# Low parts of the experts' weights by accumulating DMAs instead of subtractions in a Fourier filter with a mixture of experts

## The chip, the cores and the metric

The kernel runs on one core of a Trainium2 chip. The metric is the time of one execution on the device in microseconds (us). The names of the engines are those of the profile: PE is TensorE (PEld its weight loads), DVE is VectorE, ACT is ScalarE, POOL is GpSimd, SP is SyncE, which here only issues DMAs. ACT and POOL issue DMAs as well.

## What is computed

Eight sequences of 3072 tokens with 256 channels are filtered by a circular convolution (a real Fourier transform, a product with a filter, the transform back). The result, 24576 tokens, goes through a mixture of 8 experts: each token goes to the expert with the largest logit, an expert takes its first 768 tokens, and each token that was kept leaves as its gate weight times the expert's two-layer network. All other rows of the output are zero.

```python
X = np.fft.rfft(x, axis=1)
y = np.fft.irfft(X * (filt_r + 1j * filt_i)[None], n=x.shape[1], axis=1)
x = y.reshape(B * S, D)
logits = x @ w_gate                      # 8 experts
expert_idx = np.argmax(logits, axis=1)   # disp[e]: the first 768 rows of expert e
h = np.maximum(np.einsum('ecd,edf->ecf', disp, w1), 0.0)   # 256 -> 1024
y = np.einsum('ecf,efd->ecd', h, w2)                       # 1024 -> 256
out[i] = gate_w[i] * y[expert_idx[i], pos[i]]              # rows that were kept
```

## The kernel before

The convolution is worked out for three of the eight batches only, since the experts are full by then (a guarded second path does the rest if they are not). A batch goes through `Conv.a` and `t` (the forward transform), then `middle`, which works through six groups `g` of frequencies: `b` multiplies by the filter (DVE L267, POOL L271 and L272), `g` and `bi` transform back. `ti` and `ai` finish the transform; `ai` copies its banks to tiles `rt` (five buffers, ACT L355) and writes them to DRAM (`ybuf`, SP L359). `route` works out on DVE which token stands in which slot of which expert. In the third batch `middle` also takes pieces of other work from the list `fill`.

The experts follow. An expert has 768 slots, worked on as two chunks of 384. `prep` turns a chunk's rows, which indirect DMAs on POOL have gathered (L485), and splits them into a high part rounded to fp32r (`xh`) and a low part, the remainder (`xl`). `up` makes the hidden layer: eight steps of six matmuls of 384 columns, for the three products high by high, high by low and low by high over two halves of the 256 channels (L532, operands `wah`, `wal`, `xh`, `xl`). After each step ACT rounds the bank to the high part of `h` (L507) and DVE makes its low part (L515). `down` has three steps of 24 matmuls of 256 columns (L584, with `wbh` and `wbl`), after which ACT scales the bank into a tile `ob` (L587, four buffers) and POOL scatters its rows by an indirect DMA (L588). Matmul results go through seven PSUM banks.

The weights are split the same way, and this is what the change touches. `load_part` (L606) loads one matrix of one expert, 1 MB, as tile `raw` (part "a" is w1 with two rows of 1024 values on a partition, part "b" is w2 with eight rows of 256). It gives back the load and a list of cuts. A cut rounds its share of the columns to the high part on ACT (L621) and subtracts the high part from `raw` on POOL (L622), in one case on DVE. Experts 0 and 1a are cut into four pieces a matrix (512 columns), the later ones into two (1024 columns). There is one `raw` buffer at first (`raw0`), two later. Where the cuts stand:

- expert 0, part a: in `fill` of the third batch's `middle` (L786 to L788), one piece each in four places; the gathers of the first rows (`early_rows`) stand between the first and the second
- expert 0, part b: `run(cut_b)` at L811, between the two halves of `ai`; behind it SP loads expert 1's part a into the same buffer (L813)
- expert 1, part a: `run(cut_a)` at L824; part b: in `up` of later chunks (L847, L849)
- expert 2 and later: in `up` of the second chunk of the expert before, after every second step (L640, L571), or between down steps (L863)

All instructions of an engine run in the order in which the program issues them (`manual_schedule`).

Of the kernel before, what the change touches and what calls it, by code (L numbers as in the profile page):

```python
# [9 lines left out]
F32 = mybir.dt.float32  # L10
# [3 lines left out]
ALU = mybir.AluOpType  # L14
AF = mybir.ActivationFunctionType
# [63 lines left out]
def fftconv_moe_kernel(ctx, tc, x, fr, fi, fny, wg, w1, w2, ca, cai, cb, out, cap):  # L79
    nc = tc.nc  # L80
# [525 lines left out]
    def load_part(e, part, raw, pool, parts=2, dma=None):  # L606

        src = w1[e].rearrange("(k p) f -> p k f", p=128) if part == "a" else w2[e].rearrange("(k p) d -> p k d", p=128)
        shape = [128, src.shape[1], src.shape[2]]
        h, l = (pool.tile(shape, F32R, name="w" + part + c, tag="w" + part + c, bufs=1) for c in "hl")  # L610
        W.setdefault(e, [None] * 4)[slice(0, 2) if part == "a" else slice(2, 4)] = [h, l]
        box = []

        def load():
            box.append(raw.tile(shape, F32, name="raw", tag="raw"))
            (dma or nc.scalar).dma_start(out=box[0], in_=src)

        def cut(k, eng=None):
            w = shape[1] * shape[2] // parts
            r, fh, fl = (t.rearrange("p n f -> p (n f)")[:, k * w:(k + 1) * w] for t in (box[0], h, l))  # L620
            nc.scalar.copy(fh, r)  # L621
            (eng or nc.gpsimd).tensor_tensor(out=fl, in0=r, in1=fh.bitcast(F32), op=ALU.subtract)  # L622
        return load, [lambda eng=None, k=k: cut(k, eng) for k in range(parts)]

    def load_w(e, raw, pool):
        (la, sa), (lb, sb) = (load_part(e, part, raw, pool) for part in "ab")
        return [la, lb], sa + sb
# [69 lines left out]
    with tc.manual_schedule():  # L697
# [27 lines left out]
        fill, ahead = [[cv.finish_low]], []  # L725
        nz = -(-len(zfill) // NB0)

        def with_zeros(fill, at):
            fill = [list(f) for f in fill] + [[] for _ in range(10 - len(fill))]
            for i in range(nz):  # L730
                fill[at[i % len(at)]].append(lambda: zero_out(1))
            return fill
# [9 lines left out]
        for b in range(NB0 - 1):  # L742
            for c in range(4):
                cv.load_x(b + 1, c)
            cv.middle(V, with_zeros(fill, (2, 4, 6, 8)), ahead)
            L = new_L()
            halves = [ai(V, ybuf[b], h, L) for h in range(2)]
            counts, sums, slots, masks, table = route(L, False, (ohp, ohp))
            for q in range(4):
                ti(V, q)  # L750
            run(rows_in(b + 1, range(4), True))
            run(halves[0])
            interleave(rows_in(b + 1, range(4, 8), False), counts)
            sums()
            interleave([lambda k=k: cv.t(k) for k in range(NP // 4)], slots)
            if b + 2 == NB0:
                side_ctx.close()
                w0 = run_ctx.enter_context(tc.tile_pool(name="w0", bufs=1, side="right"))
                raw0 = run_ctx.enter_context(tc.tile_pool(name="raw0", bufs=1, side="right"))
                ep = run_ctx.enter_context(tc.tile_pool(name="ep", bufs=1, side="right"))  # L760
                (load_a, cut_a), (load_b, cut_b) = (load_part(0, part, raw0, w0, 4, nc.sync) for part in "ab")
                load_a()
            interleave(halves[1][:6], masks[:2])
            ahead = halves[1][6:]
            fill = [[table[0], masks[2]], [table[1], masks[3]], [table[2]], table[3:]]
# [19 lines left out]

        fill[2].append(cut_a[0])  # L786
        fill[3].append(early_rows)
        fill += [[cut_a[1]], [lambda: cut_a[2](nc.vector)], [cut_a[3], load_b]]  # L788
        cv.middle(V, with_zeros(fill, (2, 3, 4, 5)), ahead, last=[early_turn])
        top_ctx.close()  # L790
        w1p = run_ctx.enter_context(tc.tile_pool(name="w1p", bufs=1, side="right"))
# [18 lines left out]
        run(first[6:])  # L810
        run(cut_b)  # L811
        load_a, cut_a = load_part(1, "a", raw0, w1p, 4, nc.sync)
        load_a()  # L813
        run(counts)
# [28 lines left out]
        load_b, cut_b = load_part(1, "b", raw, w1p)  # L843
# [6 lines left out]
        load_a, cut_a = load_part(2, "a", raw, w0)  # L850
# [7 lines left out]
        load_b, cut_b = load_part(2, "b", raw, w0)  # L858
# [112 lines left out]
```

## Time and profile before

| | us |
|---|---|
| median of three runs | 520.05 |
| the three runs | 518.13, 520.05, 520.68 |
| the profiled execution | 519.1 |
| its span, from the first to the last instruction | 517.3 |
| PE busy | 493.3 (95%) |
| DVE, ACT, POOL busy | 245.7, 251.5, 243.2 (48%, 49%, 47%) |

The profile was taken of one execution. Busy times are sums over instructions; PE's matmuls overlap, so that one that is listed with 342 ns may start 170 ns after the one before. The granted clock is the share of full speed at which PE was let run: 1.00 is 2.4 GHz and 0.50 is 1.2 GHz. Times in the timeline count from the start of the span. Three batches of the convolution take the first 200 us, the experts the rest.

### The profile page before, as it was taken

How to read it: one execution, taken by the hardware profiler on the slowest of the kernel's cores; microseconds unless marked ns; L12 is line 12 of the kernel's file. 1: busy time of each engine (PE TensorE's matmuls, PEld its weight loads, DVE VectorE, ACT ScalarE, POOL GpSimd, SP SyncE). 2: the span in 40 equal slices, each digit the busy share in tenths (PEclk: the TensorE clock that was granted, in tenths of full speed). 3: DMA queues.
4: the chain of work that ended last, by engine and by line, in shares of the span. 5: the costliest groups of instructions: out<-in, count | busy, mean ns of one | idle time of the engine just before them, and what ended most of it. 6: DMA issues, size and time to landing. Idle time of an engine off the chain costs nothing.

```text
span 517.3 us, 10377 instructions
## 1 busy us (share of the span) xinstructions
PE 493.3 (95%) x4076; PEld 484.7 (94%) x4076; DVE 245.7 (48%) x532; ACT 251.5 (49%) x603; POOL 243.2 (47%) x247
## 2 busy tenths in 40 slices
PE   8999999999999988799699999999999999999995
PEld 7989999999999888799698999999999999999995
DVE  0197744887557876952434234333342342333510
ACT  2535768356674657652335256235354362353421
POOL 2165110461104765538454478558367475673012
PEclk9999999999999999979899999999999999999999
DMA  8999770996818970574130344160160340611001
GB/s 226 318 339 406 257 210 17 246 406 241 236 41 284 406 255 12 159 204 130 49 125 22 108 153 143 42 238 22 42 238 32 91 167 32 204 56 54 10 23 46
DMA packets 52923, 81.32 MB, mean 157 GB/s; under 512 B 3969, under 2 KB 31873, under 8 KB 52737
## 3 DMA queue, kind: packets, MB, share of 16 engines
q1 hardware_dynamic: 39344, 53.95, 32.2%
q10 hardware_dynamic: 8912, 13.63, 8.2%
q0 software_dynamic: 4608, 12.98, 7.3%
q8 instruction: 34, 0.56, 0.5%
q14 instruction: 25, 0.20, 0.1%
HBM read 39.07 MB, written 41.48 MB: 156 GB/s over the span
## 4 chain that ended last, share of the span: by engine, by line
PE 72%; issue 9%; POOL 6%; DVE 5%; ACT 4%; DMA 3%; POOLq 0%; SPq 0%; ACTq 0%; DVEq 0%
PE ps L532 20%; PE ps L584 20%; PE ps L227 9%; PE ps L353 6%; PE ps L284 5%; PE ps L298 4%; PE ps L251 4%; POOL y L588 2%; DMA ybuf<-rt 2%; PE ps L499 1%; POOL wbl L622 1%; DVE t L267 1%; ACT Q L243 1%; DVE V L342 1%; DMA xt<-x 1%
## 5 line engine op out<-in xcount | busy, mean ns | idle before, releaser
L584 PE MATMUL ps<-wbh,h 128*128 128x256 f32 x768 | 139.7, 282 | 0.6 <-POOL h L513 0.6
L584 PEld LDWEIGHTS ps<-wbh,h 128*128 128x128 f32 x768 | 118.9, 189 | 1.4 <-POOL h L513 1.0
L515 DVE SCALAR_TENSOR_TENSOR h<-ps,h 128x384 fp32r<-128x384 f32 x120 | 65.6, 557 | 96.8 <-ACT h L507 89.1
L584 PE MATMUL ps<-wbl,h 128*128 128x256 f32 x384 | 107.7, 280 | 0.0
L532 PE MATMUL ps<-xh,wah 128*128 128x384 f32 x256 | 87.7, 342 | 4.5 <-ACT xh L507 4.5
L507 ACT ACTIVATE h<-ps 128x384 fp32r<-128x384 f32 x128 | 61.9, 497 | 56.7 <-PE ps L532 48.1
L532 PE MATMUL ps<-xl,wah 128*128 128x384 f32 x256 | 87.7, 343 | 0.7 <-DVE xl L517 0.5
L588 POOL DMA_INDIRECT y<-ob,idxs x48 | 47.7, 994 | 84.7 <-ACT ob L587 78.8
L532 PE MATMUL ps<-xh,wal 128*128 128x384 f32 x256 | 87.3, 341 | 0.0
L584 PEld LDWEIGHTS ps<-wbl,h 128*128 128x128 f32 x384 | 72.5, 189 | 0.0
L587 ACT ACTIVATE ob<-ps,gt 128x256 f32<-128x256 f32 x48 | 22.7, 473 | 82.1 <-PE ps L584 69.1
L271 POOL TENSOR_TENSOR t<-t,t 128x256 f32<-128x256 f32 x33 | 25.1, 759 | 63.2 <-DVE t L267 59.2
L532 PEld LDWEIGHTS ps<-xh,wah 128*128 128x128 f32 x256 | 49.1, 192 | 4.9 <-ACT xh L507 4.8
L353 PE MATMUL ps<-V,AI 128*96 128x144 f32 (+1 forms) x384 | 49.4, 287 | 1.6 <-DVE V L342 1.5
L532 PEld LDWEIGHTS ps<-xl,wah 128*128 128x128 f32 x256 | 48.9, 191 | 1.6 <-DVE xl L517 1.6
L353 PEld LDWEIGHTS ps<-V,AI 128*96 128x96 f32 x384 | 47.6, 168 | 2.3 <-ACT full L512 1.8
L532 PEld LDWEIGHTS ps<-xh,wal 128*128 128x128 f32 x256 | 49.0, 191 | 0.0
L485 POOL DMA_INDIRECT rows<-ybuf,idxg x42 | 42.4, 1011 | 12.5 <-issue 11.7
L622 POOL TENSOR_TENSOR wbl<-raw,wbh 128x1024 fp32r<-128x1024 f32 (+1 forms) x18 | 38.9, 2185 | 14.0 <-ACT wbh L621 13.9
L622 POOL TENSOR_TENSOR wal<-raw,wah 128x1024 fp32r<-128x1024 f32 (+1 forms) x19 | 37.6, 1998 | 16.6 <-issue 9.3
L287 ACT CAST yh<-ps 128x408 fp32r<-128x408 f32 x48 | 24.0, 500 | 42.8 <-PE ps L284 42.5
L517 DVE TENSOR_TENSOR xl<-ps,xh 128x384 fp32r<-128x384 f32 x30 | 15.1, 546 | 59.6 <-ACT xh L507 42.6
(119 smaller groups left out, 786.8 us busy)
## 6 DMA issues: line engine op xcount, KB each, us to landing
y<-zt SPq DMA_DIRECT2D x12, 2048.0 KB, 20.4
raw<-w ACTq DMA_DIRECT2D x13, 1024.0 KB, 9.6
xt<-x SPq DMA_DIRECT2D x20, 384.0 KB, 5.1
ybuf<-rt SPq DMA_DIRECT2D x30, 162.0 KB, 2.9
ybuf<-rt SPq DMA_DIRECT2D x24, 192.0 KB, 3.7
raw<-w SPq DMA_DIRECT2D x3, 1024.0 KB, 5.7
V<-x SPq DMA_DIRECT2D x4, 384.0 KB, 8.3
AI<-cai SPq DMA_DIRECT2D x1, 1536.0 KB
```

The costliest lines, as they stand in the source:

```text
L227: nc.tensor.matmul(ps[:, i * w:(i + 1) * w], xt[:, i, h * 128:(h + 1) * 128], A[:, i * QP:i * QP + w], start=True, stop=True)
L271: eng.tensor_tensor(out=t1[:, :, 0, :], in0=t1[:, :, 0, :], in1=t2[:, :, 1, :], op=ALU.subtract)
L284: nc.tensor.matmul(ps[:, i * 136:(i + 1) * 136], self.ysb[(p // 4, h)][:, (p % 4) * 128:(p % 4 + 1) * 128], self.IG[:, h, :], start=True, ...
L287: nc.scalar.copy(fh[:, o], ps[:, :408])
L353: nc.tensor.matmul(ps[:N1, i * w:(i + 1) * w], AI[:, n0 + i, :], V[h][:, :, n0 + i, :], start=True, stop=True)
L485: nc.gpsimd.indirect_dma_start(out=rows[:, t, :], out_offset=None, in_=yrows[:lim, :], in_offset=bass.IndirectOffsetOnAxis(ap=idx[:, j + t ...
L507: nc.scalar.activation(out=hi, in_=ps, func=f)
L515: nc.vector.scalar_tensor_tensor(out=lo, in0=ps, scalar=0.0, in1=hi.bitcast(F32), op0=ALU.max, op1=ALU.subtract)
L532: nc.tensor.matmul(ps[:, :n * 128], w[:, kk, m * 128:(m + 1) * 128], y[:, kk, o], start=k == 0, stop=k == 5)
L584: nc.tensor.matmul(ps[:, :D], y[:, m, o], w[:, m, :], start=m == 0 and j == 0, stop=m == NF - 1 and j == 2)
L588: ins = nc.gpsimd.indirect_dma_start(out=out, out_offset=bass.IndirectOffsetOnAxis(ap=(idxs if ix is None else ix)[:, j:j + 1], axis=0), i ...
L622: (eng or nc.gpsimd).tensor_tensor(out=fl, in0=r, in1=fh.bitcast(F32), op=ALU.subtract)
```

## The change

A cut no longer subtracts. ACT writes the rounded high part as before, and then writes the negative of the rounded value into the low tile, by a second ACTIVATE with scale -1. Whenever the cuts have covered half of a matrix, a DMA issued by POOL reads that half of the weights (512 KB) from DRAM once more and adds it onto the low tile, which leaves the remainder there. For part "a" such a half is one row of 1024 values on each of 128 partitions, for part "b" four rows of 256. The cut that ran on DVE runs like the others. Both `tensor_tensor` forms are gone; the tile `raw` is now read by ACT alone.

```diff
-        def cut(k, eng=None):
+        def cut(k):
             w = shape[1] * shape[2] // parts
             r, fh, fl = (t.rearrange("p n f -> p (n f)")[:, k * w:(k + 1) * w] for t in (box[0], h, l))
             nc.scalar.copy(fh, r)
-            (eng or nc.gpsimd).tensor_tensor(out=fl, in0=r, in1=fh.bitcast(F32), op=ALU.subtract)
-        return load, [lambda eng=None, k=k: cut(k, eng) for k in range(parts)]
+            nc.scalar.activation(out=fl, in_=r, func=AF.Copy, scale=-1.0)
+            if (k + 1) * 2 % parts == 0:
+                n = shape[1] // 2
+                o = slice((k * 2 // parts) * n, (k * 2 // parts + 1) * n)
+                nc.gpsimd.dma_start(out=l[:, o, :], in_=src[:, o, :], accum_op=ALU.add)
+        return load, [lambda k=k: cut(k) for k in range(parts)]
...
-        fill += [[cut_a[1]], [lambda: cut_a[2](nc.vector)], [cut_a[3], load_b]]
+        fill += [[cut_a[1]], [cut_a[2]], [cut_a[3], load_b]]
```

## Rows read from the trace of the kernel before

**Rows 1.** The page, part 1: busy us, share and instructions of each engine.
```profile
PE 493.3 (95%) x4076; PEld 484.7 (94%) x4076; DVE 245.7 (48%) x532; ACT 251.5 (49%) x603; POOL 243.2 (47%) x247
```
**Rows 2.** Waits of PE: for whom, us in total, times, longest.
```profile
PE ps L532 <- ACT xh L507: 4.5, 2, 3.6
PE ps L284 <- POOL t L272: 3.9, 4, 2.0
PE pr L410 <- DVE sc L406: 3.1, 1, 3.1
```
**Rows 3.** Windows: stretch, length, busy us of each engine, clock, DMA share, GB/s.
```profile
157.00:198.00 41.00, 38.01 (x339) 36.82 (x338) 32.62 (x64) 21.40 (x73) 24.17 (x29) 1.00 0.79 280
198.00:245.00 47.00, 41.70 (x318) 40.06 (x317) 28.81 (x66) 25.21 (x58) 28.36 (x26) 0.93 0.47 136
245.00:262.00 17.00, 13.10 (x66) 12.24 (x66) 6.65 (x17) 7.37 (x15) 8.21 (x6) 0.80 0.17 48
262.00:511.00 249.00, 247.81 (x1882) 246.00 (x1880) 84.98 (x213) 106.46 (x216) 137.88 (x105) 1.00 0.29 95
```
**Rows 4.** Weight splits, by tile: duration ns min/median/max, first and last start, forms.
```profile
L622 POOL TENSOR_TENSOR wal<-raw,wah x19: 1273/2404/2438, 171.8 to 457.8; 128x1024 fp32r<-128x1024 f32 x12, 128x512 fp32r<-128x512 f32 x7
L621 ACT CAST wah<-raw x20: 622/1040/1071, 165.5 to 455.9; 128x1024 fp32r<-128x1024 f32 x12, 128x512 fp32r<-128x512 f32 x8
```
**Rows 5.** Timeline of POOL, 171 to 183 us: start, length, instruction, idle before it.
```profile
171.82 1.28 POOL L622 TENSOR_TENSOR wal<-raw,wah 128x512 fp32r<-128x512 f32 x1
...
174.63 1.18 POOL L485 DMA_INDIRECT rows<-ybuf,idx  x1 [0.17 <-DVE te L603]
...
179.85 1.27 POOL L622 TENSOR_TENSOR wal<-raw,wah 128x512 fp32r<-128x512 f32 x1
...
182.22 0.71 POOL L272 TENSOR_TENSOR t<-t,t 128x256 f32<-128x256 f32 x1
```
**Rows 6.** Timeline of PE at the longer wait for POOL in `middle`.
```profile
182.99 1.43 PE L284 MATMUL ps<-IG,t 128*128 128x136 f32 x10 [1.96 <-POOL t L272]
```
**Rows 7.** One line of `route` on DVE, the three batches: ns min/median/max.
```profile
L388 DVE TENSOR_TENSOR sc<-L,mx x3: 421/422/1478, 76.1 to 213.7; 96x256 f32<-96x256 f32 x3
```
**Rows 8.** Timeline of ACT and of SP's issues around `run(cut_b)`.
```profile
212.95 2.18 ACT L621 CAST wbh<-raw 128x512 fp32r<-128x512 f32 x4
...
225.64 1.96 ACT L355 COPY rt<-ps 96x512 f32<-96x512 f32 x3 [8.10 <-DMA ybuf<-rt]
...
219.19 0.39 SPq L616 DMA_DIRECT2D raw<-w  x1
```
**Rows 9.** Timeline at expert 1's part a: its cuts on ACT, its first use.
```profile
231.22 2.23 ACT L621 CAST wah<-raw 128x512 fp32r<-128x512 f32 x4
...
241.86 0.34 PE L532 MATMUL ps<-xh,wal 128*128 128x384 f32 x1
```
**Rows 10.** Timeline at expert 1's part b: its last cut on ACT, its first use.
```profile
259.06 1.04 ACT L621 CAST wbh<-raw 128x1024 fp32r<-128x1024 f32 x1
...
265.56 0.28 PE L584 MATMUL ps<-wbh,h 128*128 128x256 f32 x1
```
**Rows 11.** PE's longest wait, and a window (columns as in rows 3) behind it.
```profile
253.75 0.69 PE L532 MATMUL ps<-xh,wah 128*128 128x384 f32 x1 [3.59 <-ACT xh L507]
...
256.00:258.00 2.00, 2.00 (x8) 2.00 (x7) 0.66 (x2) 0.49 (x1) 0.00 (x0) 0.50 0.00 0
```
**Rows 12.** Timeline of ACT in the experts: one bank of `up`, one of `down`.
```profile
312.29 0.49 ACT L507 ACTIVATE h<-ps 128x384 fp32r<-128x384 f32 x1 [0.55 <-PE ps L532]
...
325.26 0.48 ACT L587 ACTIVATE ob<-ps,gt 128x256 f32<-128x256 f32 x1 [2.37 <-PE ps L584]
```
**Rows 13.** DMA issues (KB, median us to landing); POOL's own time for an indirect one (ns).
```profile
raw<-w SPq DMA_DIRECT2D x3, 1024.0 KB, 5.7
ybuf<-rt SPq DMA_DIRECT2D x24, 192.0 KB, 3.7
L485 POOL DMA_INDIRECT rows<-ybuf,idxg x42: 997/1002/1048, 241.1 to 451.3; - x42
```

## Prediction

> **What bounds the kernel now.** I read the busy times first: PE is busy 95% of the span, each other engine about half [rows 1]. So time can only come from stretches in which PE waits or is slowed. Cutting the span into stages shows where these are: from 262 to 511 us PE is idle 1.2 of 249 us at full clock, so the experts proper are bound by PE; between 157 and 262 us it is idle 3.0 + 5.3 + 3.9 = 12.2 us, and two parts of that run below full clock [rows 3]. Then PE's waits by cause: three rows carry nearly all of it, POOL's products in `middle` (3.9 us), the routing chain on DVE (3.1) and ACT's `xh` (4.5) [rows 2]. Last I followed each engine's timeline through those 105 us, asking what would be late next. The change can gain only there, and can lose only where a low part would come later than PE needs it.
>
> **What leaves.** POOL loses its 37 subtractions, 19 for w1 and 18 alike for w2: 26 of 2.40 us and 11 of 1.28, 76.5 us [rows 4]. One on DVE goes too. In the experts nothing waits for them, as PE doesn't idle there: worth nothing by itself.
>
> **What comes on ACT.** 38 more ACTIVATEs of the same size as the 38 roundings, 26 of 1.04 and 12 of 0.62 us: 34.5 us [rows 4]. In the experts PE fills a bank of `up` every 0.49 + 0.55 = 1.04 us [rows 12]. Where cuts stand after every second step, ACT has now 2 x 0.49 + 2 x 1.04 = 3.06 us of work for 2.08 us of PE, four times over, so it falls at most 4 us behind. Seven banks hold what up to seven steps make, and behind `up` stands `down`, whose banks come only every 2.85 us and cost 0.48 [rows 12]; ACT catches up there. Cost taken: 0. If banks did run out, 4 x 1.0 us for each of the last five experts, 20 us, would be the price.
>
> **What comes on POOL.** 32 DMAs. No direct DMA from POOL stands in this trace. The nearest is the indirect one, 1.00 us for 128 rows [rows 13] and 0.3 us to the next. I take 1.3 us for a half of w1, which is 128 runs; for a half of w2, 512 runs, between 1.3 and four times 1.0, 4.3 with the gap. An expert then has 12 x 1.3 + 2 x 1.3 + 2 x (1.3 to 4.3) = 21 to 27 us on POOL of the 2 x 8 x 1.04 + 6 x 2.85 = 33.7 us that PE takes. Behind the DMAs on POOL are the scatters of `down`, which stood behind 9.6 us of subtractions until now; `ob` has four buffers of 2.85 us. No cost.
>
> **How long such a DMA takes** no row shows. On SP 192 KB land after 3.7 us and 1024 KB after 5.7 [rows 13], so 2.4 ns a KB; 512 KB would land after 4.5 us. If adding moves the bytes twice, 1.2 us more: 5.7. With POOL's own time ahead of it, 6.7 for w1 and 9.7 for w2. So w1's half lands 4.5 to 6.7 us after POOL takes it up, w2's 4.5 to 9.7. I take the middles, 5.6 and 7.1. The Trainium skill has a price in "DMA: Bandwidth & Descriptors", section "Anatomy of one DMA — SWDGE (gpsimd) path": 2.0 us plus the bytes at 436 GB/s, an estimate of 3.2 us; by it no wait below would be left and the sum would be 1.3 us lower. No row here has such a DMA.
>
> **Gain in `middle`.** PE waits until 182.99 for POOL's product that ends at 182.93 [rows 5, 6]. Ahead of that stand, on POOL, a subtraction at 171.82, two products, three gathers from 174.63, two products, a subtraction at 179.85 and two products. Without the first subtraction all of this comes 1.25 us earlier (the index of the gathers is ready on DVE by then), so the second pair of products ends at 178.6. In place of the second subtraction (1.27) stands the first accumulating DMA (1.3), then the last pair, 0.7 each: 181.3 instead of 182.93. Gain 1.6 us; 2.9 if the issue were free, 0 if it took 3 us. What is late next is DVE, which loses its own subtraction right there, and ACT, which has 2.4 us of cuts where it had 1.2, with idle time behind them: both just keep up. Taken: -1.6.
>
> **Around `run(cut_b)`.** PE's wait of 3.1 us for the routing chain comes from DVE: L388 takes 1.48 us beside POOL's subtractions against 0.42 in other batches [rows 2, 7]. This stretch goes away. But I don't count it: what is late next is ACT, which stands 8.1 us for a free `rt` until 225.64 [rows 8], and its in-order work from there (three copies, the split of the rows, three banks of h) sets PE's next stage. That wait is for SP's writes, queued behind the load of expert 1's w1, which is issued at 219.19, when POOL has freed `raw` [rows 8]. Now ACT frees it: eight operations from 212.95 at 0.55 end at 217.4, 1.8 us earlier. Against that, an accumulating DMA beside the load: by 2.4 ns a KB 1.2 us for the half that overlaps, up to 4.9 for both halves moving twice. So ACT goes on between 1.8 us earlier and 3.1 later; taken, as the DMA engines are idle when the first half starts, -0.6.
>
> **Two low parts that may be late.** Expert 1's w1: ACT starts at 231.22, eight operations end at 235.7, POOL takes up the second half at 235.8; with 5.6 us it lands at 241.4, and PE needs it at 241.86 [rows 9]. All of this moves together, so 0 is taken; 0.6 us of wait at 6.7, no gain at 4.5. Expert 1's w2: the last cut starts at 259.06 and now ends at 261.1, POOL takes up the DMA at 261.2, it lands at 268.3; PE starts `down` at 265.56 and needs the second half 12 matmuls of 2.85/24 us later, at 267.0 [rows 10, 12]. Wait 1.3 us; between 0 and 3.9. Expert 0's two matrices and those of experts 2 to 7 have 4 us and more to spare (a w1 half of a later expert is taken up some 20 us ahead of its use).
>
> **Sum.** 519.1 (a span of 517.3 and 1.8 around it) - 1.6 - 0.6 + 0 + 1.3 = 518.2 for the profiled execution, which lies 0.95 under the median: 519.15, told as 519.2. With the bounds, from 519.15 - 1.3 - 1.2 - 1.3 = 515.4 to 519.15 + 1.6 + 3.7 + 0.6 + 2.6 = 527.7 if all ends fell together.
>
> **Rivals.**
> - *Late landings* (slower). The place is PE at 241.86 and 267.0. From a landing of about 8 us for w2 the waits eat both gains. With w2 at 9.7, w1 at 6.7 and the writes behind the load 3.1 us late: 519.15 + 2.6 + 0.6 + 3.7 = 526.1. For it: no cover at either place. Against: both times lie at the end of what the rows allow.
> - *The wait for `xh` closes* (faster). PE stands 3.59 us until 253.75 and then runs at clock 0.50 up to about 260 [rows 11] (the three windows from 254 to 260 read the same): 6 us at half speed give back 3.0. POOL reaches the gathers for that chunk 1.4 us earlier, since 2.6 us of DMA issues replace 5.0 of subtractions. If that ends the wait 1.4 us sooner and PE keeps its clock: 519.15 - 4.4 = 514.8. Against: the gathers aren't named as what ACT waits for.
> - *POOL or its DMA queue becomes the bound* (much slower). With over 4.5 us on POOL for each of the four DMAs, 12 x 1.3 + 4 x 4.5 passes the 33.7 us of an expert; at 6 us, five experts lose 4 x 1.5 each: 549. Against: 128 rows cost 1.00 [rows 13].
> - *The issue in `middle` is held up by DVE.* The gather at 174.63 took 1.18 us beside a busy DVE, others 1.00 [rows 5, 13]; a hold of 1.6 us more takes the whole gain there: 520.75. The Trainium skill's "SBUF — State Buffer" states such a rule ("The DVE blocks DMA trap", section "SBUF: two separate sides"): DMAs of GpSimd can't write their descriptors while VectorE runs certain copies; the rows show 0.18 us of it at most.
>
> **How the numbers follow.** Chances: forecast 0.47, late landings 0.21, wait closes 0.22, POOL bound 0.05, held issue 0.05. About 0.5% (2.6 us) is what a measurement of this kernel tells from no change. Faster by more: the closing wait and 0.08 of the forecast's case, where landings are as quick as the lower bound: 0.30. Slower by more: late landings nearly whole and POOL bound: 0.25. The rest, 0.45, is within. The range reaches to both neighbours, 514.0 to 526.5, and leaves out about 0.15.
>
> **What would show it.** Right: POOL's busy time down by 10 to 45 us and ACT's up by 34; PE at the product in `middle` at 181 and not 183; L388 at 0.42 in all batches while ACT still waits for `rt` close to 225; the experts at 249 us without idle PE. Wrong: PE waiting for a DMA at L532 or L584, a direct DMA on POOL over 4.5 us, or PE idle inside the experts.

## The result and the profile after

The changed kernel takes 522.16 us (median of 12 runs, 521.16 to 525.65), the kernel before on the same chip 519.35 (12 runs). The ratio is 1.0060, 95% interval 1.0041 to 1.0079: slower by 0.6%, where 519.2, no change, was forecast. The profiled execution took 521.2 us, its span is 519.3, 2.0 more than before.

The page of the changed kernel, part 1 (against [rows 1]) and two queues of part 3 (packets, MB, and the time that the packets took as a share of the span of 16 DMA engines):

```profile
PE 490.8 (95%) x4076; PEld 481.8 (93%) x4076; DVE 239.4 (46%) x531; ACT 280.0 (54%) x641; POOL 203.2 (39%) x242
...
q0 software_dynamic: 15360, 29.76, 27.0%
q10 hardware_dynamic: 8912, 13.63, 8.1%
```

POOL gave up 40 us and ACT took on 28.5, as meant. The price is on the DMA engines: q0, the queue of POOL's DMAs, was 4608 packets, 12.98 MB and 7.3% before. One of its 32 new DMAs, which adds one half of a matrix, is called an adding half below. PE's waits (for whom, us in total, times, longest), against [rows 2]:

```profile
PE ps L532 <- ACT rt L355: 6.7, 1, 6.7
PE ps L284 <- POOL t L272: 2.8, 3, 1.7
PE ps L532 <- ACT xh L507: 2.8, 2, 1.8
...
PE ps L584 <- DMA wbl<-w: 1.4, 1, 1.4
PE ps L532 <- DMA wal<-w: 1.3, 1, 1.3
```

The wait for the routing chain is gone. A wait of 6.7 us for ACT's `rt` has come, and two waits for low parts that are still on their way. The windows of [rows 3] again (length, busy us of PE, PEld, DVE, ACT, POOL, clock, DMA share, GB/s):

```profile
157.00:198.00 41.00, 38.90 (x345) 37.80 (x344) 31.86 (x66) 24.77 (x81) 21.88 (x28) 1.00 0.91 305
198.00:245.00 47.00, 36.60 (x291) 34.47 (x289) 23.32 (x62) 26.85 (x58) 21.03 (x21) 0.93 0.68 155
245.00:262.00 17.00, 14.41 (x80) 13.80 (x81) 7.11 (x18) 8.92 (x17) 6.86 (x7) 0.90 0.57 148
262.00:511.00 249.00, 246.42 (x1867) 244.51 (x1867) 84.46 (x214) 128.25 (x242) 108.01 (x104) 1.00 0.61 147
```

`middle` is better by 0.9 us, the stretch from 198 to 245 worse by 5.1 (PE busy 36.60 instead of 41.70), the one to 262 better by 1.3. In the experts only the one wait for `wbl` is added, though the DMA share doubled from 0.29 to 0.61. PE's timeline after, the starts that answer to rows of before:

```profile
181.68 1.43 PE L284 MATMUL ps<-IG,t 128*128 128x136 f32 x10 [1.71 <-POOL t L272]
...
228.00 0.69 PE L532 MATMUL ps<-xh,wah 128*128 128x384 f32 x1 [6.67 <-ACT rt L355]
...
235.44 0.50 PE L584 MATMUL ps<-wbh,h 128*128 128x256 f32 x2 [0.35 <-POOL h L513]
...
245.32 0.41 PE L532 MATMUL ps<-xh,wal 128*128 128x384 f32 x1 [1.26 <-DMA wal<-w]
...
255.33 0.45 PE L532 MATMUL ps<-xh,wah 128*128 128x384 f32 x1 [1.79 <-ACT xh L507]
...
265.99 0.28 PE L584 MATMUL ps<-wbh,h 128*128 128x256 f32 x1
...
269.07 0.35 PE L584 MATMUL ps<-wbl,h 128*128 128x256 f32 x1 [1.38 <-DMA wbl<-w]
```

One row of PE's timeline of the kernel before is needed beside them:

```profile
233.39 0.50 PE L584 MATMUL ps<-wbh,h 128*128 128x256 f32 x2 [0.34 <-POOL h L513]
```

This is the ledger of the change, as the start after less the start before: -1.31 at the product in `middle` (181.68 against [rows 6]), +2.05 where POOL's `h` lets `down` go on (235.44 against 233.39), +3.46 at the second low half of expert 1's w1 (245.32 against [rows 9]), +1.58 behind the wait for `xh` (255.33 against [rows 11]), +0.43 at expert 1's `down` (265.99 against [rows 10]), and 2.0 from the wait for `wbl` to the end. Two losses, of 3.4 and of 1.4 us, at the second and third place, a third of 1.6 at the end, 1.38 of it a wait, and two gains between.

The first loss is seen on ACT (timeline after, against [rows 8]), and on SP's queue:

```profile
211.81 0.62 ACT L621 CAST wbh<-raw 128x512 fp32r<-128x512 f32 x1
212.34 0.63 ACT L622 ACTIVATE wbl<-raw 128x512 fp32r<-128x512 f32 x1
...
215.99 2.49 ACT L355 COPY rt<-ps 96x512 f32<-96x512 f32 x5
227.36 0.58 ACT L355 COPY rt<-ps 96x512 f32<-96x512 f32 x1 [8.88 <-DMA ybuf<-rt]
228.37 1.28 ACT L355 COPY rt<-ps 96x512 f32<-96x512 f32 x2 [0.42 <-DMA ybuf<-rt]
229.55 0.49 ACT L507 ACTIVATE xh<-ps 128x384 fp32r<-128x384 f32 x1
...
216.11 0.39 SPq L616 DMA_DIRECT2D raw<-w  x1
```

The load of expert 1's w1 is issued 3.1 us earlier than before (216.11, not 219.19), and still ACT gets its next `rt` 1.7 us later: from that issue to `rt` it is 11.25 us instead of 6.45. The reason stands on POOL's timeline just ahead, and in the DMA engines' load (windows of the same kernel, columns as above):

```profile
214.31 1.40 POOL L626 DMA_DIRECT2D wbl<-w  x1 [7.11 <-ACT wbl L622]
216.38 1.30 POOL L626 DMA_DIRECT2D wbl<-w  x1 [0.68 <-ACT wbl L622]
...
235.80 0.87 POOL L626 DMA_DIRECT2D wal<-w  x1 [0.41 <-ACT wal L622]
237.88 0.87 POOL L626 DMA_DIRECT2D wal<-w  x1 [1.21 <-ACT wal L622]
...
262.63 1.31 POOL L626 DMA_DIRECT2D wbl<-w  x1 [9.14 <-ACT wbl L622]
```

```profile
214.00:222.00 8.00, 7.33 (x67) 6.79 (x65) 6.91 (x24) 4.48 (x10) 2.70 (x2) 1.00 0.73 150
222.00:230.00 8.00, 2.00 (x6) 2.00 (x7) 1.78 (x5) 2.09 (x5) 0.00 (x0) 0.71 1.14 261
...
214.00:216.00 2.00, 2.00 (x22) 2.00 (x21) 1.21 (x4) 2.00 (x6) 1.40 (x1) 1.00 0.05 8
216.00:218.00 2.00, 2.00 (x21) 2.00 (x20) 1.86 (x9) 2.00 (x6) 1.30 (x1) 1.00 0.63 75
218.00:220.00 2.00, 2.00 (x23) 1.79 (x22) 1.83 (x8) 0.48 (x1) 0.00 (x0) 1.00 1.23 202
```

From 222 to 230 us the engines are full (a share above 1, 1.14 here, means that the times of packets overlap) and PE is idle for 6 of 8 us, at a mean granted clock of 0.71. Load, writes and two adding halves go through the same engines; queue by queue, this stretch reads (DMA view of 212 to 232 us, packets, MB, share of 16 engines):

```profile
q1 hardware_dynamic: 4183, 3.00, 55.0%
q0 software_dynamic: 1056, 1.05, 34.3%
```

The two adding halves take 34.3% of 20 us, 6.9 us of all 16 engines.

### The profile page after: what moved, and what is told of

Read it like the earlier page. It is cut to its first block, busy times and chain, and to the rows that moved or that the text cites. A ratio compares the mean times of both kernels' runs of the same rounds, so it can differ in the third digit from the quotient of the medians.

```text
span 519.3 us, 10429 instructions
## 1 busy us (share of the span) xinstructions
PE 490.8 (95%) x4076; PEld 481.8 (93%) x4076; DVE 239.4 (46%) x531; ACT 280.0 (54%) x641; POOL 203.2 (39%) x242
## 4 chain that ended last, share of the span: by engine, by line
PE 67%; issue 11%; POOL 6%; DVE 6%; DMA 5%; ACT 3%; POOLq 0%; SPq 0%; DVEq 0%; ACTq 0%
PE ps L584 18%; PE ps L532 18%; PE ps L227 9%; PE ps L353 7%; PE ps L284 5%; PE ps L298 4%; PE ps L251 4%; DMA ybuf<-rt 2%; POOL y L588 2%; DVE t L267 2%; DVE V L342 1%; DMA y<-ob,idxs 1%; DMA wbl<-w 1%; PE ps L499 1%; ACT Q L243 1%
## 5 line engine op out<-in xcount | busy, mean ns | idle before, releaser
L515 DVE SCALAR_TENSOR_TENSOR h<-ps,h 128x384 fp32r<-128x384 f32 x120 | 64.4, 556 | 107.3 <-ACT h L507 102.5
L507 ACT ACTIVATE h<-ps 128x384 fp32r<-128x384 f32 x128 | 60.3, 496 | 48.2 <-PE ps L532 43.6
L353 PE MATMUL ps<-V,AI 128*96 128x144 f32 (+1 forms) x384 | 46.9, 278 | 1.8 <-DVE V L342 1.5
L353 PEld LDWEIGHTS ps<-V,AI 128*96 128x96 f32 x384 | 45.1, 160 | 2.4 <-ACT full L512 1.8
L355 ACT COPY rt<-ps 96x432 f32<-96x432 f32 (+2 forms) x57 | 29.7, 555 | 25.9 <-DMA ybuf<-rt 14.7
L284 PE MATMUL ps<-IG,t 128*128 128x136 f32 x288 | 38.2, 281 | 3.0 <-POOL t L272 2.8
L227 PEld LDWEIGHTS ps<-A,xt 96*128 96x128 f32 x320 | 38.5, 202 | 1.6 <-issue 1.6
```

The lines of the kernel that those rows point to most:

```text
L227: nc.tensor.matmul(ps[:, i * w:(i + 1) * w], xt[:, i, h * 128:(h + 1) * 128], A[:, i * QP:i * QP + w], start=True, stop=True)
L284: nc.tensor.matmul(ps[:, i * 136:(i + 1) * 136], self.ysb[(p // 4, h)][:, (p % 4) * 128:(p % 4 + 1) * 128], self.IG[:, h, :], start=True, ...
L353: nc.tensor.matmul(ps[:N1, i * w:(i + 1) * w], AI[:, n0 + i, :], V[h][:, :, n0 + i, :], start=True, stop=True)
L355: nc.scalar.copy(rt[:, :n * w], ps[:N1, :n * w])
L507: nc.scalar.activation(out=hi, in_=ps, func=f)
L515: nc.vector.scalar_tensor_tensor(out=lo, in0=ps, scalar=0.0, in1=hi.bitcast(F32), op0=ALU.max, op1=ALU.subtract)
```

## The experiments

Theory: the loss sits at two places, (a) expert 0's part b, whose adding halves share the engines with a load and with the writes that ACT waits for, and (b) expert 1's low parts, which land after PE needs them. Rivals: the added ACTIVATEs on ACT; the doubled traffic in the experts; the order of SP's queue alone. All ratios are to the kernel before on the same chip.

| kernel | adding DMAs for | median | before there | ratio, 95% |
|---|---|---|---|---|
| changed | all | 522.16 | 519.35 | 1.0060 (1.0041 to 1.0079) |
| e1 | experts 0, 1 | 522.33 | 519.82 | 1.0056 (1.0025 to 1.0086) |
| e2 | experts 2 to 7 | 519.52 | 519.82 | 0.9982 (0.9961 to 1.0002) |
| e3 | all but 0b | 519.08 | 519.82 | 0.9984 (0.9964 to 1.0005) |
| e4 | none, negatives only | 517.48 | 519.82 | 0.9955 (0.9937 to 0.9972) |
| e5 | all, copying | 518.05 | 519.65 | 0.9974 (0.9950 to 0.9999) |
| e6 | kernel before, load later | 519.69 | 519.65 | 1.0002 (0.9982 to 1.0021) |
| e7 | all, load later | 520.50 | 519.65 | 1.0021 (0.9997 to 1.0044) |
| e8 | expert 0, load later | 519.68 | 519.65 | 1.0007 (0.9988 to 1.0027) |
| e9 | all but expert 1 | 520.90 | 520.03 | 1.0019 (1.0001 to 1.0036) |
| e10 | all, 0b's cuts earlier | 523.21 | 520.03 | 1.0066 (1.0044 to 1.0088) |
| e11 | kernel before, 0b's cuts earlier | 524.94 | 520.03 | 1.0088 (1.0061 to 1.0115) |
| e12 | all, 0b's and 1a's cuts earlier | 529.88 | 520.03 | 1.0175 (1.0135 to 1.0216) |
| e13 | 0a, experts 2 to 7 | 513.00 | 514.37 | 0.9987 (0.9970 to 1.0004) |
| e14 | 0a | 511.80 | 514.37 | 0.9979 (0.9951 to 1.0007) |

**Which part of the change loses: e1, e2, e3.** Each keeps the subtractions where its condition doesn't hold. The diff is that of e1; e2 has `e >= 2` in place of `e < 2`, and e3 `(e, part) != (0, "b")`:

```diff
-            nc.scalar.activation(out=fl, in_=r, func=AF.Copy, scale=-1.0)
-            if (k + 1) * 2 % parts == 0:
+            if e < 2:
+                nc.scalar.activation(out=fl, in_=r, func=AF.Copy, scale=-1.0)
...
+            else:
+                (nc.vector if (e, part, k) == (0, "a", 2) else nc.gpsimd).tensor_tensor(out=fl, in0=r, in1=fh.bitcast(F32), op=ALU.subtract)
```

> Only experts 0 and 1 get their low parts by negation on ACT and accumulating DMAs; experts 2 to 7 are subtracted on POOL as before. Theory (the loss arises before 270 us, where accumulating DMAs share the DMA engines with the load of expert 1's w1 and the writes of ybuf, and where expert 1's low parts land late): as slow as the changed kernel, 2 to 3.5 us over the kernel before, with ACT's wait for a free rt of 8 to 9 us, ending near 227, and PE waiting for DMA at wal and wbl. Rival (the second reading of the weights costs time in the experts): within 1 us of the kernel before.

> Only experts 2 to 7 are changed; experts 0 and 1 are subtracted as before. Theory: within 1 us of the kernel before, PE without idle time from 262 us on, although POOL's busy time falls and ACT's rises as far as in the changed kernel for these experts. Rival (traffic or ACT's extra work in the experts): 2 us or more over the kernel before.

> The changed kernel, but expert 0's w2 (the cuts between the two halves of ai) is subtracted on POOL as before. Theory (two accumulating DMAs beside the load and the ybuf writes hold up ACT's rt by about 5 us): ACT's wait for rt ends some 1.3 us earlier than in the kernel before, near 224 us, DVE's L388 takes 1.4 to 1.5 us again, and the time is 0 to 1.5 us under the kernel before, 3 to 4 us under the changed one. Rival (ACT's added instructions make the loss): ACT keeps most of them, so 1.5 us or more over the kernel before.

e1 is as slow as the changed kernel and e2 is not slower than the kernel before: all of the loss comes from experts 0 and 1, and the rival of the traffic in the experts falls. e3, with one matrix of sixteen put back, is level with the kernel before: expert 0's part b carries most of it. ACT and SP in e3:

```profile
224.58 1.96 ACT L355 COPY rt<-ps 96x512 f32<-96x512 f32 x3 [8.13 <-DMA ybuf<-rt]
...
218.09 0.39 SPq L616 DMA_DIRECT2D raw<-w  x1
```

From the load's issue to `rt` it is 6.49 us, as before (6.45); with the adding halves it was 11.25.

**What the adding DMAs do: e4 and e5.** e4 leaves the DMAs out, e5 lets them copy; in both the low parts are not the remainders that the computation needs.

```diff
-            if (k + 1) * 2 % parts == 0:
...
-                nc.gpsimd.dma_start(out=l[:, o, :], in_=src[:, o, :], accum_op=ALU.add)
```

```diff
-                nc.gpsimd.dma_start(out=l[:, o, :], in_=src[:, o, :], accum_op=ALU.add)
+                nc.gpsimd.dma_start(out=l[:, o, :], in_=src[:, o, :])
```

> The changed kernel without its accumulating DMAs: ACT still writes the rounded and the negated rounded values, but the weights aren't added, so the low parts are wrong and so is the output. Theory: the wait for rt ends about 6.5 us after SP's load of expert 1's w1, near 222.5 us, no wait for a DMA at wal or wbl, and the time is 2 to 5 us under the kernel before. Rival (ACT's 38 added ACTIVATEs make the loss): still 1 to 3 us over the kernel before.

> The changed kernel, whose DMAs on POOL copy the weights into the low tile instead of adding them (the low parts are left out of the computation by it). Same bytes read from DRAM, same issues on POOL. Theory (an adding DMA occupies the DMA engines about twice as long as a copy, and so delays the load and the writes at 217 to 230): a 4 KB packet of that queue takes about 0.2 us instead of 0.34, ACT's wait for rt ends about 2 us earlier (near 225.5 instead of 227.4), the median is 519.5 to 520.8. Rival (the price is that of 512 KB more on the engines, whatever is done with them): the rt wait ends within 0.5 us of 227.4, the median stays at 521.5 to 522.5.

e4 has all of ACT's added work and is the fastest of its comparison: ACT's 38 ACTIVATEs are not the loss, and that rival falls. Its load is issued at 214.81 and the next `rt` comes at 221.47, 6.66 us later. e5 (timeline of ACT, and its queue on the page):

```profile
226.49 1.94 ACT L355 COPY rt<-ps 96x512 f32<-96x512 f32 x3 [8.21 <-DMA ybuf<-rt]
```

```profile
q0 software_dynamic: 15360, 29.76, 19.8%
```

The load is issued at 215.91, so 10.58 us to `rt`: copying the same 1 MB costs 4.1 us there, adding it 4.8 and another 0.4 behind. My expectation, that `rt` would come 2 us earlier than with adding, was half wrong (it came 0.9 earlier, and the median of 518.05 lies below what either side named): at this place it is the bytes that cost, and adding little more. But PE's waits for `wal` and `wbl`, 1.26 and 1.38 us, are gone with copies, and the median fell by over 4 us against the changed kernel: that adding is slower shows where a low part is awaited. With the share of q0 as packet time of all 16 engines, less the 37.8 us (7.3% of 517.3) that it had before, 32 halves take 102.4 us added (27.0% of 519.3) and 64.8 copied (19.8% of 517.9): 3.2 and 2.0 us a half.

**Whether the order of SP's queue is enough: e6, e7, e8.** The load of expert 1's w1 goes behind five of the eight steps that write `ybuf`; e8 adds for expert 0 only.

```diff
         load_a, cut_a = load_part(1, "a", raw0, w1p, 4, nc.sync)
-        load_a()
         run(counts)
         run(rest[:5])
+        load_a()
```

> The kernel before; only the issue of expert 1's load of w1 on SP stands behind the second half of ai instead of ahead of it, so that the writes of ybuf are no longer queued behind 1 MB. Theory (what sets the stretch is the wait for rt, and that is the writes behind the load): the rt wait of 8.1 us shrinks to under 3 us and ends before 222, and the median falls by 1.5 to 3 us, 516.5 to 518, unless the load itself is late for ACT's cuts at 231. Rival (the writes are slow by themselves, or the wait for xh takes all of it): within 0.7 us of the kernel before.

> The changed kernel with the same move of the load. Theory (three parties share the DMA engines from 217 to 230, and the load is the one of them that stood ahead of the writes): the rt wait ends before 223 instead of at 227.4, and the median falls by 2 to 4 us, to 518 to 520; the wait for the low part of expert 1's w1 stays at 1 us or grows, since the load lands later. Rival (the adding DMAs alone hold up the writes): the rt wait still ends after 225.5, and the median is over 520.7.

> Adding DMAs for expert 0 only, subtractions on POOL for all others (so no wait for a low part of expert 1), and the load moved as in the run before. Theory (two separate losses, the rt wait and the late low parts): both are gone, the 1.3 us of middle and the 0.42 us at L388 are kept, median 516 to 518, below both kernels and below the kernel before with the move alone. Rival (the wait for xh takes up what the others give back): no better than 518.5.

The theory's number for e6 was wrong. ACT no longer waits for the writes, yet its `xh` comes only 1.1 us earlier (226.44 against 227.50), since PE, which has stood 3.0 us for the routing chain, delivers its banks late. ACT's timeline of e6:

```profile
222.54 0.58 ACT L355 COPY rt<-ps 96x512 f32<-96x512 f32 x1 [4.96 <-PE ps L353]
...
225.96 0.58 ACT L355 COPY rt<-ps 96x512 f32<-96x512 f32 x1 [1.13 <-PE ps L353]
226.44 0.49 ACT L507 ACTIVATE xh<-ps 128x384 fp32r<-128x384 f32 x1
```

So in the kernel before two chains end close together at this place: the writes behind the load (225.64), and the slowed PE. Taking away the first gains 1.1 us, and this is gone where PE next waits for `xh`, until 253.94 in e6 and 253.75 before. In e7, where the routing chain is on time, the move brings ACT's `xh` from 229.55 to 227.21 and the median is 0.4% lower against before, 520.50 where 518 to 520 was expected: ACT still stands twice for `rt` (3.97 us until 222.46, 2.95 until 225.99), the load is then late for its own cuts (1.75 us at 232.87), PE stops for 1.61 us at the second low half of w1, and waits 1.0 for `wbl`. e8, expected at 516 to 518, shows no gain over the kernel before: with adding halves for expert 0 alone, `rt` still waited 3.46 and 3.49 us.

**Whether the adding halves can be put elsewhere: e10, e11, e12.** `run(cut_b)` and the load go ahead of the first half of `ai`, in the changed kernel (e10) and in the one before (e11); e12 also moves expert 1's `run(cut_a)` to the place that became free.

```diff
         run(early[:5])
+        run(cut_b)
+        load_a, cut_a = load_part(1, "a", raw0, w1p, 4, nc.sync)
+        load_a()
...
         run(first[6:])
-        run(cut_b)
-        load_a, cut_a = load_part(1, "a", raw0, w1p, 4, nc.sync)
-        load_a()
```

> The changed kernel with the cuts of expert 0's part b and the load of expert 1's part a moved some 10 us ahead, in front of the first half of ai, so that the two adding DMAs and the load run before the writes of the second half. Theory (the loss at rt is contention among these three at 217 to 230): the rt wait of 8.9 us shrinks to under 3 us and ends before 222.5, POOL's xl gate comes 3 to 6 us earlier, the wait for wal stays near 1.3 us, and the wait for xh grows; median 517 to 520. Rival (the writes of ybuf are slow whatever stands beside them): the rt wait still ends after 225, median over 521.

> The kernel before with the same move of the cuts and of the load. Theory (in the kernel before the routing chain on DVE and the half clock behind it end no earlier than the rt wait, as in the run with the late load): POOL's subtractions now stand ahead of the gathers of the second early rows and away from L388, which drops to 0.42 us; PE's 3.1 us at L410 go, the rt wait too, and the wait for xh takes back most of it; 517 to 519.5. Rival: no change, 519.3 to 520.

> As the run of the changed kernel with the early cuts, and the cuts of expert 1's part a moved too, to the old place of expert 0's part b. Theory (the second loss is a low part that lands 7.4 us after its DMA is taken up, without cover): PE's wait for wal is gone; but these two adding DMAs now stand beside the writes of ybuf again, without the load, so the rt wait ends between 222 and 225; median 516.5 to 519, below both kernels. Rival (adding DMAs beside the writes are enough for the whole loss): rt wait ends after 226, median 520 or more.

None of the three went as I expected; I had looked at the second half of `ai` and forgotten that the first half writes `ybuf` too. ACT and SP in e10, and in e11, where nothing adds:

```profile
215.67 0.52 ACT L355 COPY rt<-ps 96x432 f32<-96x432 f32 x1 [8.17 <-DMA ybuf<-rt]
218.14 0.51 ACT L355 COPY rt<-ps 96x432 f32<-96x432 f32 x1 [1.96 <-DMA ybuf<-rt]
...
205.46 0.40 SPq L616 DMA_DIRECT2D raw<-w  x1
```

```profile
215.99 0.52 ACT L355 COPY rt<-ps 96x432 f32<-96x432 f32 x1 [8.22 <-DMA ybuf<-rt]
...
209.10 0.40 SPq L616 DMA_DIRECT2D raw<-w  x1
```

From the load's issue to the next `rt` it is 6.89 us in e11 and 10.21 in e10. The same holds in every run in which the 1 MB load stands ahead of writes of `ybuf` on SP: 6.4 to 6.9 us with no adding half beside it (the kernel before, e2, e3, e4, e11, e13, e14), 10.2 to 11.3 with two adding halves (changed, e1, e9, e10, e12). Put into the first half of `ai`, the load also holds up the routing chain, and PE stands 7.7 to 9.1 us at L353. e12 went the rival's way: beside writes of `ybuf` without the load, w1's adding halves still hold up `rt` by 2.78 us until 231.66 and 2.67 until 234.91.

**Whether the second place is a loss of its own: e9, e13, e14.** Conditions in the diff of e1: `e != 1`; `e >= 2 or (e, part) == (0, "a")`; `(e, part) == (0, "a")`.

> The changed kernel with expert 1's two matrices split by subtractions on POOL as before; all other low parts by adding DMAs. Theory (two separate losses: ACT's wait for rt, and PE's two waits of 1.26 and 1.38 us for expert 1's low parts): the rt wait still ends near 227.4, the waits of PE for wal and wbl are gone, and the wait for xh takes back a part of the first; median 519.5 to 521.5. Rival (all of the loss is the rt wait, the two waits are covered by later ones): 522 or more.

> Adding DMAs for expert 0's part a and for experts 2 to 7; expert 0's part b and both parts of expert 1 by subtractions on POOL as before. Theory (two places are the whole loss): the rt wait ends near 224.5 and not at 227.4, no wait of PE for wal or wbl, the middle keeps its gain of 1.1 to 1.3 us, of which the wait for xh may take a part: 0.7 to 1.5 us below the kernel before, 518.2 to 519.2. Rival (a third loss is left, from the traffic in the experts): no better than the kernel before, 519.5 or more.

> Adding DMAs for expert 0's part a alone, all others by subtractions. Theory (the traffic of experts 2 to 7 costs nothing): within 0.4 us of the run with adding DMAs in the experts. Rival: faster than that one by over 0.8 us, as the experts are then as before.

In e9 the wait for `rt` is unchanged (226.78 and 227.87), the waits for `wal` and `wbl` are gone, PE's longest wait for `xh` is back at 3.59, and the ratio falls from 1.0060 to 1.0019. So expert 1's low parts cost 0.41%, 2 us, and expert 0's part b (1.0060 against 0.9984 in e3) 0.76%, 4 us, each to some 0.3%. e13 undoes both and is 0.13% under the kernel before, e14 0.21%, both intervals reaching just past 1: no third loss shows, and what is left of the gain is too small for these runs to tell from nothing. Between e13 and e14 the question stays open: the ratios differ by 0.4 us, as the theory had it, the medians by 1.2 us, as the rival had it, and seven runs of e14 lie at 511 to 512 us, the other five at 514 to 517. The two losses don't add up: undone together they give back 0.73%, no more than the first alone. One reason is in e3, where PE's stops at `wal` and `wbl` have shrunk to 0.68 and 0.99 us although expert 1 still adds. How much it explains isn't settled, as e13 and e14 ran on another chip (there the kernel before takes 514.37 us, and PE waited only 0.96 us for `xh` in both). No version that computes everything beat both kernels by more than its interval.

## Why the prediction failed, step by step

- **`middle`, -1.6**: right in kind, 0.3 too large. The product came 1.31 us earlier; the wait is down from 1.96 to 1.71. Two errors offset each other: the gathers moved up by only 0.64 us, not 1.25 (173.99 against [rows 5]), and the first adding half held POOL's next product for 0.65 us (179.19 to 179.84), not 1.3.
- **POOL's issue**: right. A half of w1 takes 0.95 us (1.3 taken), a half of w2 1.31, the lower end of 1.3 to 4.3. The rival of POOL as the bound was never near, and the held issue was not there: in `middle` the two halves of w1 took 1.00 and 1.29 us, and beside a busy DVE two of w2 took 1.40 and 1.30, in the experts 1.31. That doesn't test the rule of the Trainium skill ("SBUF — State Buffer", section "SBUF: two separate sides") that the prediction weighed, which is on operations of VectorE such as fp32 copies within SBUF: the only copy that DVE ran beside the two of w2 was one of 96x8 values out of a matmul's bank (L415).
- **ACT in the experts, 0, and the experts at full speed**: right (e2). ACT's busy time rose by 28.5 us and not by 34: neighbours overlap (a length of 0.62 us at 211.81, the next start at 212.34), and busy time counts an overlap once, so it is not the plain sum of the lengths.
- **L388**: right, 0.42 us in all batches, and PE's wait of 3.1 us went.
- **Around `run(cut_b)`, -0.6**: this is the step that failed. `xh` came 2.05 us later (229.55 against 227.50) although the 1.31 us of `middle` had reached this place, so the term was +3.4: of the other sign, and just past the bound of +3.1. The earlier issue of the load was right: of its 3.08 us, 1.14 came with the start of ACT's first cut (211.81 against [rows 8]) and 1.94 from the cuts, 1.8 taken. Mis-sized was the cost of the adding halves beside it: I charged 1.2 us for the half that overlaps, on the ground that the engines are idle when the first one starts. They measured 4.8 us, close to the 4.9 that I had kept for the bound, both halves moving twice. The ground was true and of no use: the share is 0.05 from 214 to 216 us, but the first half is only taken up at 214.31, and by the time its bytes move the load is issued (216.11). The trace of before had what was needed: the engines were already full behind the load (share 1.02 from 222 to 230 us), so another 1.05 MB at the 293 GB/s of that window is worth an estimate of 3.6 us; copying did cost 4.1 (e5). The window of the kernel before:

```profile
222.00:230.00 8.00, 8.00 (x52) 7.66 (x51) 6.27 (x20) 4.15 (x10) 1.55 (x2) 0.74 1.02 293
```

- **Expert 1's w1, 0**: a wait of 1.26 us. The second half was taken up by POOL at 237.88 and awaited until 245.32, 7.4 us; 5.6 were taken, 6.7 was the upper bound. Both halves go through one queue 2.08 us apart, and one takes 3.2 us of all engines (e5's working), so by this estimate the second starts about 1.1 us late; I had priced each half as if alone. That the whole place came later is not the reason: POOL took the half up 2.1 us later than in my working (235.8), and PE reached the place 2.2 us later (244.06 against 241.86).
- **Expert 1's w2, +1.3**: right in kind, and at 1.38 in size too, the size partly by luck: POOL took the half up 1.4 us later than I had it (262.63, not 261.2), the landing was 0.7 shorter (6.44 us, 7.1 taken), and PE needed it 0.7 later.
- The price in the Trainium skill ("DMA: Bandwidth & Descriptors", section "Anatomy of one DMA — SWDGE (gpsimd) path"), by which neither wait would be left, does not hold for these: 6.4 and 7.4 us here, against the estimate of 3.2.
- **The rival of the closing wait** came true in part and for another reason: the wait shrank from 3.59 to 1.79 us, because PE came 3.4 us later to it and its end moved by only 1.6, and the half clock behind it was shorter (0.52, 0.63 and 1.00 in the three windows from 256 to 262 us; 0.50, 0.50 and 0.92 before). It gave back 1.88 and then 1.15 us of the ledger. In e4 PE came 4.3 us earlier than in the kernel before and waited 6.44 us, until 252.29. Of ACT's gaps ahead of `xh` there, the last two have no releaser on this core by name (timeline of e4), so what sets this time stays open:

```profile
242.01 1.05 ACT L621 CAST wbh<-raw 128x1024 fp32r<-128x1024 f32 x1 [2.40 <-DMA raw<-w]
...
248.11 0.49 ACT L507 ACTIVATE h<-ps 128x384 fp32r<-128x384 f32 x1 [0.96 <-remote]
250.98 0.49 ACT L507 ACTIVATE h<-ps 128x384 fp32r<-128x384 f32 x1 [2.38 <-remote]
```

The sum with what was measured at the failed steps: 517.3 - 1.3 + 3.4 + 1.4 for the two losses to 245 us, -3.0 at `xh`, +1.4 at `wbl` gives 519.2, the span after being 519.3; as these are differences of one ledger, that they meet shows only that no piece is left out. Late landings, the rival with 0.21, is the case that came nearest: its places were right, with the writes behind the load as its largest part.

## What to carry to other kernels

Work that is moved from an engine to a DMA is paid where other DMAs stand on the path, not by the average load: charge its bytes against the rate of that stretch, and look up whether the engines are already full there. Here, doubling the traffic for 249 us of experts cost nothing that the runs show, 1 MB of it in one full stretch cost 4 us. Use the adding DMA for weights that are loaded well ahead, and keep the subtraction where the low part is needed within some 8 us (6.4 and 7.4 were waited here) or where a write gates an engine.

## What was not expected of the hardware

- By the time of its packets, an adding half of 512 KB takes 3.2 us of all 16 DMA engines, a copied one of the same shape 2.0, and one of ACT's 1 MB loads (q10: 8.1% of 519.3 us for 13) 3.2 us for twice the bytes. So a byte that is added took about twice the engine time of one that is loaded.
- POOL's own time for the issue depends on adding: 0.95 and 1.31 us for the halves of w1 and w2 (means of 16), 0.58 and 0.77 for the same as copies (e5).
